# Fused attention and token mixer on one core: g_norm as one row, batch 1 per head pair, planned SyncE issues, and u of two batches turned by DMA

## The chip, the core and the metric

The kernel runs on one core of a Trainium2 chip. The metric is the device time of one execution in microseconds. Every run of a changed kernel was made beside runs of the kernel before on the same chip. The profile of an execution shows five compute engines (PE for matmuls and transposes by matmul, DVE, ACT, POOL, and SP, which here only issues transfers) and 16 DMA engines. Two words are used below. A run is called *slow* when it took over 1.5% longer than the fastest run of the same kernel, and *fast* otherwise; slow runs are left out of all ratios, but not out of the medians. *Half clock* is something else: in these traces PE's granted clock falls to 0.50 during or after some of PE's idle times, and stays there for 3.4 or 6.8 us while the kernel runs.

## The reference, cut to what matters

```python
# B=8 batches, H=8 heads, S=576 tokens, D=64; all inputs float32
def attention(q, k, v, g_norm):
    kv  = einsum('bhsd,bhse->bhde', k, v)
    out = einsum('bhsd,bhde->bhse', q, kv)
    rms = sqrt(mean(out*out, axis=-1, keepdims=True) + 1e-6)
    return out / rms * g_norm                      # g_norm has D elements

def mixer(x, w_theta, w_tok_r, w_tok_i, w_ch):     # x: (8, 576, 512)
    theta = x @ w_theta
    yr = einsum('ts,bsd->btd', w_tok_r, x * cos(theta))
    yi = einsum('ts,bsd->btd', w_tok_i, x * sin(theta))
    u  = x + yr + yi
    return u + maximum(u @ w_ch, 0)

# reference: x = attention(...) with heads side by side, result = mixer(x, ...)
```

## The kernel before

The kernel does not write its instructions in a loop. It adds every step of all eight batches as a task to an object called `Weave`: the engines that can do it with an assumed cost, the tasks it needs, the buffers it makes and uses, a priority (`due`), and, for a transfer, an assumed DMA time. While the kernel is built, `Weave.run` plays this through on a clock of its own and emits each task when its engine takes it. What comes out is a *fixed order for each engine*. On the chip nothing is decided any more: each engine takes its instructions in that order, and if the next one is not ready, all behind it wait.

```python
class Weave:
    RATE = 0.335e6          # bytes per us: a load of 256 KB is taken to need 0.78 us
    BACKLOG = 3.5           # at most so many us of transfers queued ahead
    ...
    def run(self):
        ...
                if dma is not None:
                    at = max(at, dma_free - self.BACKLOG)
        ...
            if dma is not None:
                (first, size, packed) = dma
                begin = max(start + first, dma_free)
                dma_free = begin + size / self.RATE / packed   # one server, one after the other
                end = dma_free + 0.35
            done[name] = end
...
    SP = ("SP", 0.1, 0.1)                                      # cost of an issue on SP
...
            weave.add((kind, b, hp), [SP], due(...), part(kind, src), ...,
                      dma=dma(size, 1.0), load=True)           # q, k, v: 0.78 us
...
                          dma=dma(T * H * D * 4, 0.45), load=True)   # last 64 tokens: 0.87 us
...
            weave.add(("qT", b, j), [SP], due("turn_q", b, j), fn, ...,
                      dma=dma(128e3, 0.24))                    # DMA transpose of q: 1.59 us
...
        weave.add(("out", b, ti), [...], at, store, ...,
                  dma=dma(n * P * 4, 0.9))                     # store: 0.87 us, of the last rows 0.43
```

Per batch: loads of q, k, v by head pair; q cast to 16 bit (`qcast`, DVE) and turned by DMA transposes (`qT`); kv; raw attention product, its norm (`sq` ACT, `ss` DVE, `rt` POOL, `x` DVE); transposes of x (`xTps`); `th` = x @ w_theta; cos and sin; `z` (DVE); the token mix `y` (576 matmuls in all); `uT`; u turned back by PE (`ups`); `vps` = u @ w_ch; result `ot` and its store. PE is filled with useless matmuls (`warm`) while it has nothing to do at the head.

```python
MIX_AFTER = 5                       # the mixer weights are loaded behind this head pair
...
            for r in range(P // D):                            # g_norm as a column
                nc.gpsimd.dma_start(out=gcol[r * D:(r + 1) * D, :], in_=g_norm.unsqueeze(1))
...
            for (half, r) in parts:                            # last 64 rows: two stores
                nc.sync.dma_start(out=out[b, SF:S, r * n:(r + 1) * n], in_=t[half])
```

Of the kernel before, what the change touches and what calls it, by code (L numbers as in the profile page):

```python
# [18 lines left out]
PERIOD = 24.57  # L19
START = 4.0  # L20
DUE = {
    "load": (-15.33, 2.93),
    "theta": (25.64, 0),
    "mixers": (14.15, 5.87),
    "wch": (40.71, 0.59),
    "wT": (22.86, 0.63),
    ("phase", 0): (15.82, 0),
    ("mix", 0): (31.46, 3.57),
    ("channel", 0): (44.52, 6.51),
    "first": (-5.15, 0),  # L30
    "cast": (16.13, 1.47),
    "turn_q": (5.73, 0),
    "attention": (1.6, 3.69),
    "norm": (12.64, 4.53),
    "turn": (15.9, 4.83),
    "phase": (19.49, 4.62),
    "mix": (45.0, 2.9),
    "channel": (62.48, 5.74),
# [4 lines left out]
    "rt": 6, "x": 9, "xT": 3, "pt": 2, "f": 2, "fa": 2, "tr": 2, "uT": 2, "u": 3, "ot": 3,  # L43
# [3 lines left out]
MIX_AFTER = 5  # L47
WCH_AFTER = 7


class Weave:
# [8 lines left out]
    SLACK = {"PE": 0.053, "ACT": 0, "DVE": 0.124, "POOL": 0.1, "SP": 0.05}  # L60
    MARGIN = {"PE": 0.051, "ACT": 0, "DVE": 0.444, "POOL": 0.1, "SP": 0.0}
    RATE = 0.335e6
    BACKLOG = 3.5
    BEGIN = {"PE": 1.6, "ACT": 2.2, "DVE": 1.7, "POOL": 2.5, "SP": 0.7}
    WARM = 40.0
# [19 lines left out]
    def run(self):  # L85
        done, free, last = {}, dict(self.BEGIN), {}
        dma_free = 0.0
# [21 lines left out]
        while ready:  # L109
            best = {}  # L110
            for t in ready:
                (name, engines, due, fn, needs, makes, uses, dma) = t
                if any(not self.slots[tag] for (tag, _) in makes):
                    continue
                at = max([done[n] for n in needs], default=0.0)
                for (tag, _) in makes:
                    at = max(at, min(self.slots[tag]))
                if dma is not None:
                    at = max(at, dma_free - self.BACKLOG)
                for (e, cost, lat) in engines:  # L120
                    start = max(free[e], at + self.MARGIN[e])
                    if name[0] == "warm" and start > self.WARM:
                        continue
                    best.setdefault(e, []).append((start, due, at, t, cost, lat))
            picks = []
            for (e, c) in best.items():
                first = min(x[0] for x in c) + self.SLACK[e]
                (start, due, at, t, cost, lat) = min(
# [3 lines left out]
                    (max(free[o], at) + k for (o, k, _) in t[1] if o != e), default=1e9  # L132
# [3 lines left out]
                picks.append((start, due, e, at, t, cost, lat))  # L136
            if not picks:
                break
            (_, _, e, at, t, cost, lat) = min(picks, key=lambda x: x[:3])
            (name, engines, due, fn, needs, makes, uses, dma) = t  # L140
            start = max(free[e], at)
            free[e] = start + cost
            end = start + lat
            if dma is not None:
                (first, size, packed) = dma
                begin = max(start + first, dma_free)
                dma_free = begin + size / self.RATE / packed
                end = dma_free + 0.35
# [35 lines left out]
def kernel(  # L184
# [78 lines left out]
    gcol = const.tile([P, 1], FP32, tag="gcol")  # L263
    wth = wpool.tile([P, NK, C], FP16, tag="wth", name="wth")
# [7 lines left out]
    def act(n, operands=0, small=False):  # L272
        cost = 0.1 + n / 1200.0 + 0.09 * operands
        return ("ACT", cost, cost + 0.14)

    def dve(cost):
        return ("DVE", cost, cost + 0.14)

    def pe(cost):
        return ("PE", cost, cost + 0.22)  # L280

    SP = ("SP", 0.1, 0.1)

    def dma(size, packed=1.0, first=1.7):
        return (first, size, packed)


    def idle_work(n):
# [9 lines left out]
        weave.add(("warm", n), [("PE", 0.22, 0.25)], 1e6, fn, makes=[("mm", name)])  # L298

    def load(b, hp):  # L300
        pair = slice(2 * hp, 2 * hp + 2)
        whole = P * 2 * NF * D * 4

        def part(kind, src):
            def fn(e):
                if kind == "q" or b > 0:
# [26 lines left out]
        for (i, (kind, src)) in enumerate((("q", q), ("k", k), ("v", v))):  # L333
            size = P * 2 * NF * D * 4 if kind == "q" or b > 0 else P * NS * D * 4
            weave.add((kind, b, hp), [SP], due("load", b, hp) + 0.01 * i, part(kind, src),
                      makes=[(kind, f"{kind}{b}_{hp}")], dma=dma(size, 1.0), load=True)
        if hp == (0 if b else HP - 1):
            for (i, (kind, src)) in enumerate((("kl", k), ("vl", v), ("ql", q))):
                if b == 0 and kind != "ql":
                    continue  # L340
                weave.add((kind, b), [SP], due("load", b, hp) + (0.04 if b else -0.04) + 0.01 * i,
# [4 lines left out]
                          dma=dma(T * H * D * 4, 0.45), load=True)  # L346

    def load_weights():


        def chunk(name, src, at):
            rows, cols = src.shape

            def fn(e):
# [4 lines left out]
            weave.add(name, [SP], at, fn, makes=[("wst", name)],  # L359
                      dma=dma(P * cols * 4, 1.0), load=True)  # L360

        def cast(name, of, out, src, at, scale=1.0, pool=True):
# [14 lines left out]
            on = [act(n), dve(0.06 + n / 1900.0), ("POOL", 0.17 + n / 960.0, 0.2 + n / 960.0)]  # L377
            weave.add(name, on[2:] if pool else on[:2], at, fn, needs=[of], uses=[of])
# [3 lines left out]
        for kc in range(NK):  # L382
            chunk(("wst", kc), moe_w_theta[kc * P:(kc + 1) * P, :], at + 0.01 * kc)
            cast(("wth", kc), ("wst", kc), wth[:, kc, :],
                 lambda kc=kc: st["wst", kc][:, 0:C], due("theta", 0, kc), FOLD, False)
# [17 lines left out]
        def fetch(e):  # L403
            for r in range(P // D):
                nc.gpsimd.dma_start(out=gcol[r * D:(r + 1) * D, :], in_=g_norm.unsqueeze(1))

        def gain(e):
            nc.vector.tensor_scalar(
                out=gcol[:], in0=gcol[:], scalar1=math.sqrt(D), scalar2=None, op0=ALU.mult
            )  # L410
        weave.add("gain", [("POOL", 1.3, 9.0)], -100.0, fetch)
        weave.add("gcol", [dve(0.1)], due("first", 0, 1), gain, needs=["gain"])

        def table(e):
            nc.scalar.activation(out=warm[:], in_=pio2_t[:], func=AFT.Sin)
        weave.add("sin", [("ACT", 1.5, 1.6)], due("first", 0, HP + 2), table,
                  needs=[("rt0", hp) for hp in range(HP + 1)])

    def mixer_step(n):
# [28 lines left out]
        weave.add(("wT", n), [act(S), dve(0.65)], at, keep, needs=[("wTps", n)], uses=[name])  # L448


    def cast_q(b, hp):
# [11 lines left out]
        at = due("cast", b, hp) if b else due("first", b, hp)  # L463
        weave.add(("qc", b, hp), [dve(0.33)], at, whole,
                  needs=[("q", b, hp)], makes=first,
                  uses=[f"q{b}_{hp}"] + more)
        if hp == 0:
            weave.add(("qcl", b), [dve(0.33)], at + (0.1 if b else 9.0), tail,
                      needs=[("ql", b)], uses=[f"ql{b}", f"qc{b}"])

    def turn_q(b):
        for j in range(NT):
            def fn(e, j=j):
                if j == 0:
# [6 lines left out]
            weave.add(("qT", b, j), [SP], due("turn_q", b, j), fn,  # L481
# [3 lines left out]
                      dma=dma(128e3, 0.24))  # L485

    def turn_q_by_pe(b, hp):
        name = f"qTps{b}_{hp}"
        pair = slice(2 * hp, 2 * hp + 2)

        def turn(e):
            pq = st[name] = ps("tp", [P, SX], FP16, name)
            for j in range(NT):
                nc.tensor.matmul(
                    pq[:, j * P:(j + 1) * P], qcast[b % 2][:, j, pair, :], ident16[:],
                    is_transpose=True, start=(j == 0), stop=(j == NT - 1),
                )

        def keep(e):
            if hp == 0:  # L500
                st["qT", b] = sb("qT", [P, HP, S], FP16, f"qT{b}")
            t = st["qT", b][:, hp, :]
            if e == "ACT":
                nc.scalar.copy(out=t, in_=st[name][:, 0:S])
            else:
                nc.vector.tensor_copy(t, st[name][:, 0:S])

        at = due("attention", b, hp) - 0.02
        weave.add((name,), [pe(0.3)], at, turn, needs=[("qc", b, hp), ("qcl", b)],
# [527 lines left out]
```

## Time and profile before

| | |
|---|---|
| time, median of 3 runs | 231.53 us (231.21 to 233.05) |
| span of the profiled run | 230.3 us |
| PE busy | 220.8 us, of which 23.4 us are warm matmuls |
| mean granted clock | 1.000 |
| first y / theta of batch 1 | 44.3 us / 53.8 us |

The warm matmuls of the kernel before in two stretches (0 to 25 and 25 to 60 us) and in sum; the columns are stretch, length, busy time of PE, DVE and ACT, clock, DMA share, GB/s:

```profile
0.00:25.00 25.00, 15.22 (x51) 0.06 (x1) 0.41 (x2) 1.00 0.93 261
25.00:60.00 35.00, 8.15 (x30) 0.00 (x0) 0.00 (x0) 1.00 0.99 291
sum 250.00, PE 23.38 DVE 0.06 ACT 0.41; mean PE 3.90 DVE 0.01 ACT 0.07
```

The chain of waits of the kernel before between 20 and 50 us: start, duration, what.

```profile
17.36 7.20 DMA vl<-in_v_dram
...
25.26 2.70 PE th L806 x12
...
33.41 0.87 PE wTps L432 x10
34.28 0.97 PE warm L293 x4
...
44.39 2.07 PE y L893 x18
```

The loads bound the first 25 us; after them, filler and transposes of the mixer weights (`wTps`) fill PE until the first y.

Waits of the kernel before: engine and line, what it waited for, us in total, times, longest.

```profile
DVE qcast L453 <- DMA q<-in_q_dram: 4.9, 2, 2.7
DVE qcast L459 <- DMA ql<-in_q_dram: 1.9, 1, 1.9
```

From 100 to 160 us PE is busy 59.89 of 60 us. The engines hardly ever wait for a load.

### The profile page before, as it was taken

To read this page: it belongs to the slowest core of one execution; us is meant where nothing else is said; L and a number is where in the kernel's file an instruction comes from. 1 tells how busy PE (TensorE), PEld (TensorE's weight loads), DVE (VectorE), ACT (ScalarE), POOL (GpSimd) and SP (SyncE) were. 2 spreads that over 40 slices of the span, in tenths; PEclk is the share of its full clock that TensorE was granted. 3 is DMA by queue.
4 is the path that set the end of the run, shared out by engine and by line. 5 is a ranking of instruction groups with operands and counts; after the bars stand their busy time and mean duration, and the time that the engine had idled before them with its cause. 6 is when DMAs were issued, how large, how long until landed. Compare 5 with 4: busy or idle time off the path is not lost.

```text
span 230.3 us, 5955 instructions
## 1 busy us (share of the span) xinstructions
PE 220.8 (96%) x2342; PEld 145.8 (63%) x2342; DVE 185.2 (80%) x368; ACT 157.3 (68%) x298; POOL 88.0 (38%) x108
## 2 busy tenths in 40 slices
PE   7999999999996999999999999999999999999992
PEld 2674555786754665677667766865675668655861
DVE  2268599279997798799999997998799989987553
ACT  2477687327995688767896877589849797877031
POOL 8000197436513670464266033543275336430000
PEclk9999999999999999999999999999999999999999
DMA  5899999999749996974899467996894412103214
GB/s 184 291 344 239 291 254 313 330 272 335 127 124 260 340 162 159 331 235 82 190 317 353 90 151 213 318 195 155 234 306 122 117 57 93 48 23 137 71 46 159
DMA packets 59931, 46.42 MB, mean 202 GB/s; under 512 B 29056, under 2 KB 52608, under 8 KB 59904
## 3 DMA queue, kind: packets, MB, share of 16 engines
q1 hardware_dynamic: 59840, 46.05, 71.9%
q8 instruction: 18, 0.29, 0.6%
q14 instruction: 9, 0.07, 0.1%
q0 software_dynamic: 64, 0.00, 0.0%
HBM read 33.06 MB, written 9.44 MB: 185 GB/s over the span
## 4 chain that ended last, share of the span: by engine, by line
PE 73%; DMA 9%; DVE 6%; ACT 5%; POOL 3%; issue 1%; SPq 1%; DVEq 0%
PE y L893 27%; PE vps L937 11%; PE th L806 11%; PE kv L524 6%; DMA wst<-in_moe_w_theta_dram 4%; PE xTps L775 4%; PE ups L928 4%; PE warm L293 3%; DMA vl<-in_v_dram 3%; PE raw L572 3%; DMA v<-in_v_dram 2%; POOL rt L594 2%; ACT tr L849 2%; DVE x L606 2%; PE wTps L432 2%; PE th L811 1%
## 5 line engine op out<-in xcount | busy, mean ns | idle before, releaser
L893 PE MATMUL y<-wT,z 128*128 128x320 f16 (+1 forms) x576 | 79.1, 286 | 2.2 <-DVE z L859 2.2
L893 PEld LDWEIGHTS <-z 128*128 128x128 f16 x576 | 54.0, 98 | 19.1 <-DVE z L859 2.8
L594 POOL TENSOR_TENSOR rt<-ss,mhalf 128x8 f32<-128x8 f32 x35 | 61.0, 1744 | 2.9
L590 POOL TENSOR_SCALAR ss<-ss 128x8 f32<-128x8 f32 x35 | 9.5, 271 | 85.2 <-DVE ss L583 84.6
L901 DVE SCALAR_TENSOR_TENSOR uT<-y,gcol,xT 128x256 f16<-128x256 f32 (+1 forms) x64 | 32.7, 512 | 7.9 <-PE y L893 7.6
L937 PE MATMUL vps<-wch,uT 128*128 128x512 f16 (+1 forms) x192 | 37.7, 344 | 0.0
L818 ACT ACTIVATE pt<-th,magic_t 128x512 f32<-128x512 f32 (+1 forms) x40 | 25.7, 642 | 16.6 <-PE th L806 13.3
L806 PE MATMUL th<-wth,xT 128*128 128x512 f16 x128 | 32.7, 380 | 0.0
L784 ACT ACTIVATE xT<-xTps,gcol 128x512 f16<-128x512 f16 (+1 forms) x36 | 22.9, 635 | 13.3 <-PE xTps L775 13.0
L944 ACT COPY u<-ups 128x512 f16<-128x512 f16 (+1 forms) x40 | 21.0, 537 | 14.9 <-PE ups L928 14.6
L859 DVE TENSOR_TENSOR z<-x,tr 128x1024 f16<-128x1024 f16 (+1 forms) x40 | 27.0, 674 | 3.4 <-ACT tr L849 1.7
L948 DVE SCALAR_TENSOR_TENSOR ot<-vps,u 128x512 f32<-128x512 f32 (+1 forms) x40 | 25.2, 633 | 4.1 <-PE vps L937 2.6
L822 DVE SCALAR_TENSOR_TENSOR f<-pt,th 128x512 f32<-128x512 f32 (+1 forms) x40 | 25.2, 629 | 4.0 <-ACT pt L818 3.7
L606 DVE TENSOR_TENSOR x<-raw,rt 128x512 f16<-128x512 f32 x36 | 24.7, 685 | 3.0 <-POOL rt L594 2.4
L583 DVE TENSOR_REDUCE ss<-sq 128x8 f32<-128x512 f32 x36 | 24.3, 680 | 2.3 <-ACT sq L579 2.0
L293 PE MATMUL warm<-kvbd 128*128 128x512 f16 x81 | 23.4, 410 | 2.0 <-DVE pio_t L250 1.5
L841 ACT ACTIVATE tr<-fa,pio_t 128x512 f16<-128x512 f32 x32 | 23.0, 720 | 0.5 <-DVE fa L829 0.3
L841 ACT ACTIVATE tr<-f 128x512 f16<-128x512 f32 x32 | 20.2, 630 | 3.4 <-DVE f L822 3.2
L579 ACT ACTIVATE sq<-raw 128x512 f32<-128x512 f32 x36 | 21.1, 591 | 1.2 <-PE raw L572 0.9
L937 PEld LDWEIGHTS <-uT 128*128 128x128 f16 (+1 forms) x192 | 14.1, 102 | 8.1 <-issue 0.4
L524 PE MATMUL kv<-v,k 128*64 128x64 f32 x448 | 19.0, 227 | 0.0
L524 PEld LDWEIGHTS kv<-v,k 128*64 128x64 f32 x448 | 15.3, 137 | 5.6 <-issue 4.2
(80 smaller groups left out, 243.4 us busy)
## 6 DMA issues: line engine op xcount, KB each, us to landing
q<-in_q_dram SPq DMA_DIRECT2D x32, 256.0 KB, 5.1
out_dram<-ot SPq DMA_DIRECT2D x32, 256.0 KB, 3.6
k<-in_k_dram SPq DMA_DIRECT2D x28, 256.0 KB, 5.1
v<-in_v_dram SPq DMA_DIRECT2D x28, 256.0 KB, 5.5
k<-in_k_dram SPq DMA_DIRECT2D x4, 288.0 KB, 6.2
v<-in_v_dram SPq DMA_DIRECT2D x4, 288.0 KB, 6.4
wmix<-in_moe_w_tok_r_dram SPq DMA_DIRECT2D x4, 288.0 KB, 5.5
wmix<-in_moe_w_tok_i_dram SPq DMA_DIRECT2D x4, 288.0 KB, 4.0
```

The costliest lines, as they stand in the source:

```text
L293: nc.tensor.matmul(t[:], kv_bd[1][:, 0, :], kv_bd[1][:].rearrange("p h c -> p (h c)"), start=True, stop=True,)
L524: nc.tensor.matmul(kvp[r * D:(r + 1) * D, hp, :], st["k", b, hp][:, r, j, :] if j < NF else st["kl", b][:, 2 * hp + r, :], st["v", b, hp][ ...
L594: nc.gpsimd.tensor_tensor(out=r[:], in0=t[:], in1=mhalf[:], op=ALU.pow)
L606: nc.vector.tensor_tensor(out=t[:].rearrange("p (h e) -> p h e", h=H), in0=st[raw][:].rearrange("p (h e) -> p h e", h=H), in1=st[rt][:].un ...
L806: nc.tensor.matmul(t[:], xT[:, kc, :], wth[:, kc, :], start=(kc == 0), stop=(kc == NK - 1),)
L818: nc.scalar.activation(out=t[:], in_=st[th][:], func=AFT.Identity, bias=magic_t[:])
L822: nc.vector.scalar_tensor_tensor(out=t[:], in0=st[pt][:], scalar=MAGIC, in1=st[th][:], op0=ALU.subtract, op1=ALU.subtract,)
L841: nc.scalar.activation(out=t[:, which, :], in_=src[:], func=AFT.Sin, scale=-RAD, bias=0.0 if bias is None else bias[:],)
L859: nc.vector.tensor_tensor(out=t[:], in0=xb.unsqueeze(1).broadcast_to((P, w, C)), in1=st[tr][:, 0:w, :], op=ALU.mult,)
L893: nc.tensor.matmul(t[:], z[:, kc * P:(kc + 1) * P], wT[m][:, cols], start=(m == 0), stop=(m == NM - 1),)
L901: nc.vector.scalar_tensor_tensor(out=st["uT", b][:, kc, cols], in0=st[y][:], scalar=gcol[:], in1=st["xT", b][:, kc, cols], op0=ALU.mult, o ...
L937: nc.tensor.matmul(t[half], uT(kc), wch[:, kc, r * n:(r + 1) * n], start=(kc == 0), stop=(kc == NK - 1),)
```

## The change

Its intent is to take filler out of the head, to take work off PE and DVE, and to plan SP's issues and the transfers with durations closer to those of the chip. Cut to its core:

```diff
-MIX_AFTER = 5
+U_FROM = 5
+MIX_AFTER = 3                       # mixer loads ahead of batch 1
 class Weave:
-    RATE = 0.335e6
-    BACKLOG = 3.5
-    WARM = 40.0
+    LANES = 8                        # at most 8 transfers in flight
+    WARM = 56.4
...                                    # DUE, PERIOD, SLACK, MARGIN retuned; URGENT, AHEAD added
-                    at = max(at, dma_free - self.BACKLOG)
+                    at = max(at, landed[-self.LANES])
...
-                (first, size, packed) = dma
-                begin = max(start + first, dma_free)
-                dma_free = begin + size / self.RATE / packed
-                end = dma_free + 0.35
+                (first, took) = dma
+                dma_free = max(start + first, dma_free) + took
+                end = dma_free + 0.2
+                landed.append(end)
...
-    SP = ("SP", 0.1, 0.1)
+    def sp(cost): ...                # load 0.47, tail 0.64, weights 0.38, qT 1.3, store 0.46
...                                    # assumed DMA time   before -> after
                                       # load of 256 KB      0.78 -> 0.71
                                       # load of last rows   0.87 -> 0.9
                                       # q transpose         1.59 -> 0.5
                                       # store of 256 KB     0.87 -> 0.65
                                       # weights             0.78 -> 0.66
...
-            on = [act(n), dve(...), ("POOL", ...)]
-            weave.add(name, on[2:] if pool else on[:2], ...)
+            weave.add(name, [act(n), dve(..., True), pool(n)], ...)   # any of three may cast
...
-                nc.gpsimd.dma_start(out=gcol[r * D:(r + 1) * D, :], in_=g_norm.unsqueeze(1))
+                nc.gpsimd.dma_start(out=grow[:, r * D:(r + 1) * D], in_=g_norm.unsqueeze(0))
...
+            nc.tensor.matmul(gps[:], grow[:], root_d[:], start=True, stop=True)
+            nc.vector.tensor_copy(gcol[:], gps[:])
...
-            if b == 0: first(hp) ...  # only batch 0 by head pair
+            if b < 2: by_pair(b, hp)
...
-        half, kc = divmod(i, NK)      # y: 8 chunks per batch
+        half = int(i >= NK // 2)      # y: first half in pairs of chunks, 6 per batch
+        kcs = [i - NK // 2] if half else [2 * i, 2 * i + 1]
...
-            for (half, r) in parts:
-                nc.sync.dma_start(out=out[b, SF:S, r * n:(r + 1) * n], in_=t[half])
+            nc.sync.dma_start(
+                out=out[b, SF:S, :].rearrange("t (r c) -> r t c", r=len(parts)), in_=t[:]
+            )
...
+                nc.sync.dma_start_transpose(      # u of batches 5 and 6, 8 for each
+                    out=ub[:, 2 * half:2 * half + 2, kc * P:(kc + 1) * P],
+                    in_=uT[:, kc, half * SH:(half + 1) * SH],
+                )
```

## The prediction

> **What bounds it now.** The page's busy row gives PE 96% (220.8 of 230.3 us), DVE 80%, ACT 68%. From 84 to 212 us the PE timeline is packed, so only less PE work helps there. Slack is at the head: 23.4 us of PE is filler (81 warm matmuls; windows of the warm tile put 15.2 us before 25 us, 8.2 us between 30 and 45 us), and 2.7 us idle between 60 and 80 us, on z and x of batches 1 and 2. PE work proper is about 197 us.
>
> The chain of waits at the head: loads until theta starts at 25.3, then filler and mixer transposes until the first y at 44.4. That y does not wait for z (last ends at 39.3) but for the mixers: their loads are issued after six head pairs (23.2 to 32.7 us), POOL alone casts them (28.2 to 38.6 us), the last wT ends near 43.9.
>
> **The change, costed.**
> 1. Mixer loads move ahead of batch 1, right behind theta's, and three engines may cast. At the 300 GB/s the page shows here, batch 0, theta and mixers (7 MB) take about 23 us (estimate); staging has six slots, so I put the last mixer at 29 to 31 us and the first y at 33 to 35. Batch 1's loads (11 us) come later; y of batch 0 (8.9 us), its channel stage (4.9 us) and kv by pair fill that. Filler falls from 23.4 to about 14 us: 9 us gained.
> 2. Batch 1 by head pair: same matmuls, but its norm chain starts with the first pair; takes perhaps 1 us of the 60 to 80 us bubble.
> 3. u of batches 5 and 6 by DMA: 32 PE transposes of the ups group go; four take 0.22 us start to start, so 8 tiles save 1.8 us of PE (and 8 x 0.58 us of ACT). 16 DMA transposes come; those of qT took SP 1.25 us each and landed in 2.5 us. The Trainium skill ("DMA: Bandwidth & Descriptors", DMA Transpose) asks for a two-byte type and an SP or ACT queue; both hold (30 already run here). DMA share is 0.2 to 0.7 there; SP order is the risk.
> 4. y's first half in pairs of chunks: 64 evacuations become 48. 256 columns took 0.48 us, 512 of the same operation 0.69: 16 x 0.27 = 4 us of DVE, mostly off the path.
> 5. g_norm as a row: nearly nothing; gcol's DVE operation at 13.7 us had no idle before it.
> 6. Issue planning, single tail store: at most 1 us.
>
> **Sum.** -9 -1 -1.8 -1, and 2 us given back to new waits: 231.5 - 11 = 220.5 us. Range 214 to 227.5. Chances: faster by over 2% 0.86, within 0.12, slower 0.02.
>
> **Right** if: warm matmuls fall to 12 to 16 us; the first y starts before 36 us; mixer casts end before 33 us, on ACT, DVE and POOL; the ups group has 32 fewer full-size transposes; PE from 84 us stays packed. **Wrong** if: y still starts near 44 us; warm stays above 20 us; PE idles at 45 to 60 us on batch 1's loads; a DVE ot waits for the transposes, or SP holds stores and loads behind them.
>
> **What would make it wrong:** DMA at the head slower than 300 GB/s; casts delaying batch 0's chain; a changed steady pace (about 24 us per batch), several us either way.

## More of the kernel before

The profile page of the kernel before, its busy part and its slices: busy time of each engine with its share of the span; then the span in 40 slices of 5.8 us, each digit the busy share in tenths. PEclk is the granted clock in tenths (9 is 90% or more).

```profile
span 230.3 us, 5955 instructions
PE 220.8 (96%) x2342; PEld 145.8 (63%) x2342; DVE 185.2 (80%) x368; ACT 157.3 (68%) x298; POOL 88.0 (38%) x108
PE   7999999999996999999999999999999999999992
PEclk9999999999999999999999999999999999999999
DMA  5899999999749996974899467996894412103214
```

PE is full nearly everywhere, and never at half clock. The DMA engines are full for the first 60 us and have pauses later: the loads run ahead of the work.

The steady part, all engines, in two windows: PE, PEld, DVE, ACT, POOL busy, clock, DMA share, GB/s.

```profile
60.00:100.00 40.00, 37.09 (x440) 25.20 (x439) 35.05 (x71) 31.05 (x59) 16.28 (x16) 1.00 0.90 224
100.00:160.00 60.00, 59.89 (x658) 40.88 (x657) 56.04 (x112) 46.69 (x87) 26.23 (x26) 1.00 0.77 206
```

The timeline of SP at the end shows the two stores of the last 64 rows:

```profile
226.70 1.11 SPq L960 DMA_DIRECT2D out_dram<-ot  x2
```

## The result, and the profile after

| | before | after |
|---|---|---|
| median | 232.04 us (231.21 to 233.05, 4 fast runs) | 249.73 us (247.38 to 252.28, 2 fast and 2 slow runs) |
| span of the profiled run | 230.3 us | 245.6 us |
| mean granted clock | 1.000 | 0.955 |
| warm matmuls | 23.4 us | 9.7 us |
| first y / theta of batch 1 | 44.3 / 53.8 us | 35.7 / 55.0 us |

The change made the kernel slower: the ratio is 1.0674, with a 95% interval of 1.0587 to 1.0761. A ratio here is the mean time of one kernel's fast runs over that of the other's fast runs of the same rounds, so it is not quite the ratio of the medians quoted: the two fast runs after are 247.38 and 248.08 us. The result is correct.

The profile page after:

```profile
span 245.6 us, 5784 instructions
PE 215.3 (88%) x2255; PEld 145.0 (59%) x2255; DVE 182.1 (74%) x368; ACT 151.5 (62%) x292; POOL 83.8 (34%) x98
PE   6498979999968968794999999399999999999990
PEclk9979998999999999998699999679999999999998
DMA  6997899999899969989998994639312225134432
```

PE has less to do (215.3 us instead of 220.8) and yet the span is 15.3 us longer. PE's row has holes, and in or just behind each of the three deepest (4, 4 and 3 tenths) the clock's digit is below 9. The DMA row shows fewer pauses up to 140 us than before: the loads no longer run ahead.

The warm matmuls after (the same columns), and the two steady windows:

```profile
0.00:25.00 25.00, 7.47 (x19) 0.06 (x1) 0.20 (x1) 0.93 0.88 272
25.00:60.00 35.00, 2.20 (x6) 0.00 (x0) 0.20 (x1) 0.95 1.14 288
sum 250.00, PE 9.67 DVE 0.06 ACT 0.40; mean PE 1.61 DVE 0.01 ACT 0.07
```

```profile
60.00:100.00 40.00, 33.78 (x426) 23.02 (x425) 30.32 (x60) 26.64 (x52) 12.81 (x14) 1.00 0.99 230
100.00:160.00 60.00, 51.56 (x497) 34.92 (x498) 49.18 (x97) 41.20 (x77) 27.24 (x27) 0.90 0.99 216
```

The filler did go, 13.7 us of it. But from 100 to 160 us PE is busy 51.56 us instead of 59.89 and its mean clock there is 0.90, while the DMA share rose from 0.77 to 0.99. The waits after:

```profile
DVE qcast L479 <- DMA q<-in_q_dram: 12.3, 14, 4.0
DVE qcast L485 <- DMA ql<-in_q_dram: 10.0, 5, 3.6
PE y L935 <- DVE f L855: 7.5, 2, 3.9
PE gps L430 <- DMA grow<-in_g_norm_dram: 2.6, 1, 2.6
```

DVE's waits for q (6.8 us before: 4.9 and 1.9) are 22.3 us now. How such a wait reaches PE is seen in the chain of waits after, from 108 us on:

```profile
108.45 0.29 SPq L1011
108.78 4.32 DMA q<-in_q_dram
113.13 0.43 DVE qcast L479
113.55 0.60 DVE ss L580
114.15 0.60 DVE z L892
114.75 0.61 DVE f L855
```

and in the timelines of DVE and PE of the same microseconds (start, duration, instruction, and in brackets the idle time before it with what ended it):

```profile
108.35 0.75 DVE L946 SCALAR_TENSOR_TENSOR uT<-y,gcol,xT 128x512 f16<-128x512 f32 x1
113.13 0.43 DVE L479 CAST qcast<-q 128x512 f16<-128x512 f32 x1 [4.03 <-DMA q<-in_q_dram]
...
110.76 1.03 PE L839 MATMUL th<-wth,xT 128*128 128x512 f16 x4
115.40 2.56 PE L935 MATMUL y<-wT,z 128*128 128x320 f16 x9 [3.62 <-DVE f L855]
```

SP issued the load of q only at 108.78. DVE's fixed order has the cast of that q next, so DVE stands still for 4.03 us with `ss`, `z` and `f` of another batch behind the cast, all of them ready. PE in turn waits 3.62 us for them, and the clock is 0.50 from 114.4 to 121.2 us, from within this idle time on. The same happens again at 153 us: DVE waits 3.60 us for the last rows of q of batch 7 (`ql`, issued at 149.5 us), PE waits for `f` behind that cast, and the clock is 0.50 from 155.3 to 162.2 us.

```profile
157.35 2.93 PE L935 MATMUL y<-wT,z 128*128 128x256 f16 x13 [3.88 <-DVE f L855]
```

Added over the trace, stretches of more than 0.6 us from the start of one matmul to the start of the next are 4.2 us before and 25.2 us after, and PE ran about 20 us at half clock, by which some 10 us of full clock are lost (the mean clock, 0.955 of 245.6 us, gives 11).

When the loss occurs can be read by asking when PE has done a given amount of matmul work, with filler left out. The columns are times of the kernel before; the entries are how much later (+) or earlier (-) the other kernel has done the same work.

| at (us) | 45 | 75 | 85 | 95 | 105 | 115 | 145 | 155 | 205 |
|---|---|---|---|---|---|---|---|---|---|
| after | -3.3 | -1.4 | -0.7 | +2.3 | +3.9 | +10.0 | +14.9 | +16.0 | +14.6 |

The kernel after is ahead at 45 us, loses everything between 75 and 155 us, and keeps its pace from then on. The first DMA transpose of u is issued at 186.6 us, behind the loss; no `ot` waited for one.

The end of SP's timeline after:

```profile
239.79 0.52 SPq L1015 DMA_DIRECT2D out_dram<-ot  x1
```

SP needs 0.52 us for one store instead of 1.11 us for two. But the span ends at 245.6, 5.8 us after that issue, where it ended 3.6 us after the issue before (226.70 and 230.3). The 128 packets of 1024 bytes of the last rows took from 240.95 to 244.22 us with two or three in flight; before, from 227.83 to 228.91 us with up to 16 in flight, most often 13 or 14.

### The profile page after: what moved, and what is told of

Its sections match the earlier page's. It is cut to its first block, busy times and chain, and to the rows that moved or that the text cites. A ratio compares the mean times of both kernels' runs of the same rounds, so it can differ in the third digit from the quotient of the medians.

```text
span 245.6 us, 5784 instructions
## 1 busy us (share of the span) xinstructions
PE 215.3 (88%) x2255; PEld 145.0 (59%) x2255; DVE 182.1 (74%) x368; ACT 151.5 (62%) x292; POOL 83.8 (34%) x98
## 4 chain that ended last, share of the span: by engine, by line
PE 47%; DMA 17%; SPq 13%; DVE 10%; POOL 4%; ACT 3%; issue 3%; DVEq 0%; POOLq 0%; ACTq 0%
PE y L935 19%; DMA q<-in_q_dram 9%; PE vps L993 8%; PE th L839 6%; SPq L503 6%; PE kv L521 5%; SPq L329 4%; DMA grow<-in_g_norm_dram 2%; DMA vl<-in_v_dram 2%; DMA k<-in_k_dram 2%; DVE ss L580 2%; POOL rt L591 2%; DVE ot L1004 2%; PE xTps L786 2%; PE raw L569 2%
## 5 line engine op out<-in xcount | busy, mean ns | idle before, releaser
L935 PE MATMUL y<-wT,z 128*128 128x320 f16 (+1 forms) x576 | 82.7, 295 | 9.7 <-DVE f L855 7.5
L935 PEld LDWEIGHTS <-z 128*128 128x128 f16 x576 | 56.0, 100 | 29.3 <-issue 11.3
L591 POOL TENSOR_TENSOR rt<-ss,mhalf 128x8 f32<-128x8 f32 x31 | 53.2, 1717 | 2.6
L851 ACT ACTIVATE pt<-th,magic_t 128x512 f32<-128x512 f32 (+1 forms) x40 | 25.4, 641 | 16.0 <-PE th L839 11.5
L946 DVE SCALAR_TENSOR_TENSOR uT<-y,gcol,xT 128x320 f16<-128x320 f32 (+1 forms) x48 | 29.3, 611 | 6.2 <-PE y L935 6.0
L874 ACT ACTIVATE tr<-f 128x512 f16<-128x512 f32 x32 | 19.9, 629 | 13.1 <-DVE f L855 13.1
L1000 ACT COPY u<-ups 128x512 f16<-128x512 f16 (+1 forms) x32 | 16.8, 530 | 15.9 <-PE ups L984 15.6
L479 DVE CAST qcast<-q 128x512 f16<-128x512 f32 x32 | 13.6, 428 | 13.3 <-DMA q<-in_q_dram 12.3
L603 DVE TENSOR_TENSOR x<-raw,rt 128x512 f16<-128x512 f32 x32 | 21.8, 683 | 0.8 <-POOL rt L591 0.2
L795 ACT ACTIVATE xT<-xTps,gcol 128x512 f16<-128x512 f16 (+1 forms) x32 | 20.0, 632 | 2.9 <-PE xTps L786 2.8
L1004 DVE SCALAR_TENSOR_TENSOR ot<-vps,u 128x512 f32<-128x512 f32 (+1 forms) x32 | 19.7, 617 | 2.8 <-PE vps L993 2.2
L892 DVE TENSOR_TENSOR z<-x,tr 128x1024 f16<-128x1024 f16 (+1 forms) x32 | 19.7, 616 | 0.7 <-ACT tr L882 0.3
L839 PEld LDWEIGHTS <-xT 128*128 128x128 f16 x128 | 11.6, 99 | 12.0 <-issue 1.2
```

What stands on the lines that cost most here:

```text
L591: nc.gpsimd.tensor_tensor(out=r[:], in0=t[:], in1=mhalf[:], op=ALU.pow)
L603: nc.vector.tensor_tensor(out=t[:].rearrange("p (h e) -> p h e", h=H), in0=st[raw][:].rearrange("p (h e) -> p h e", h=H), in1=st[rt][:].un ...
L839: nc.tensor.matmul(t[:], xT[:, kc, :], wth[:, kc, :], start=(kc == 0), stop=(kc == NK - 1),)
L851: nc.scalar.activation(out=t[:], in_=st[th][:], func=AFT.Identity, bias=magic_t[:])
L874: nc.scalar.activation(out=t[:, which, :], in_=src[:], func=AFT.Sin, scale=-RAD, bias=0.0 if bias is None else bias[:],)
L935: nc.tensor.matmul(st[y][:, c, :], z[:, kc * P:(kc + 1) * P], wT[m][:, cols], start=(c == 0 and m == 0) if open_sums else m == 0, stop=m = ...
```

## The experiments

The prediction had counted the planning as "at most 1 us" gained. Theories after reading the traces:

- **A.** The new assumed transfer times are too short. The planner puts casts, transposes and issues where their data will not be there yet, and as every engine works in order, one late load stops all. The head's gain is lost this way.
- **B.** The DMA transposes of u, and SP's time for them, delay stores and loads.
- **C.** The row of g_norm, which PE must wait for at 8.8 us, starts a delay that is never made good.
- **D.** The order by head pair in batch 1 does harm.
- **E.** The single store of the last rows costs at the end.

The expectations below use other letters for some of these: there B is the row of g_norm (C here), C the order by head pair (D here), and D the DMA transposes of u (B here). A is the same.

All eighteen runs gave correct results. The table gives them all. *Planned* is the start of PE's last product (of the last `vps`) on the planner's own clock, printed while the kernel is built; *chip* is the start of the same instruction in the trace; *late* is the difference. *DMA sum* is what the planner assumed for the transfers of one steady batch (12 loads, 3 loads of last rows, 5 q transposes, 4 stores and one of last rows): for the kernel before 12 x 0.7825 + 3 x 0.869 + 5 x 1.592 + 4 x 0.869 + 0.435 = 23.9 us.

| kernel | median us | ratio (95%) | DMA sum | planned | chip | late |
|---|---|---|---|---|---|---|
| before | 232.04 | 1 | 23.9 | 219.4 | 225.5 | 6.1 |
| after | 249.73 | 1.0674 (1.0587, 1.0761) | 16.7 | 209.7 | 238.6 | 28.8 |
| a_u8 | 249.53 | 1.0699 (1.0618, 1.0780) | 16.7 | 211.7 | 241.2 | 29.5 |
| a_gcol | 250.80 | 1.0779 (1.0713, 1.0845) | 16.7 | 211.4 | 247.2 | 35.8 |
| a_oldplan | 239.53 | 1.0301 (1.0236, 1.0366) | 23.9 | 220.6 | 228.2 | 7.6 |
| b_newplan | 247.74 | 1.0664 (1.0592, 1.0736) | 16.7 | 214.0 | 241.7 | 27.7 |
| a_took | 237.68 | 1.0214 (1.0172, 1.0255) | 23.9 | 219.9 | 227.0 | 7.0 |
| a_back | 247.22 | 1.0601 (1.0526, 1.0677) | 16.7 | 210.6 | 235.4 | 24.8 |
| a_op_u8 | 240.36 | 1.0253 (1.0167, 1.0340) | 23.9 | 222.1 | 232.4 | 10.2 |
| a_op_pair0 | 237.84 | 1.0224 (1.0171, 1.0277) | 23.9 | 221.4 | 227.0 | 5.6 |
| b_tail1 | 234.58 | 1.0098 (1.0068, 1.0127) | 23.9 | 219.4 | 225.9 | 6.5 |
| a_tail2 | 246.23 | 1.0563 (1.0502, 1.0624) | 16.7 | 209.7 | 239.1 | 29.3 |
| a_took_tail2 | 233.12 | 1.0048 (1.0001, 1.0094) | 23.9 | 219.9 | 225.4 | 5.4 |
| a_took_tail2_early | 235.33 | 1.0147 (1.0104, 1.0190) | 23.9 | 219.9 | 228.5 | 8.5 |
| b_mix3 | 232.82 | 1.0013 (0.9963, 1.0063) | 23.9 | 221.0 | 226.3 | 5.2 |
| a_meas | 239.88 | 1.0307 (1.0249, 1.0364) | 20.1 | 214.7 | 231.0 | 16.3 |
| n_t4 | 237.06 | 1.0193 (1.0136, 1.0250) | 20.1 | 212.4 | 230.4 | 18.0 |
| n_t2 | 237.27 | 1.0182 (1.0123, 1.0241) | 20.1 | 213.2 | 230.1 | 16.9 |
| a_took_early2 | 237.13 | 1.0177 (1.0138, 1.0217) | 23.9 | 221.9 | 229.2 | 7.3 |
| n_m2 | 231.12 | 0.9922 (0.9883, 0.9961) | 22.8 | 218.2 | 224.8 | 6.6 |

(The profiled runs of a_gcol, a_op_u8 and a_tail2 are slow ones, so their chip and late columns are too high by some microseconds; their ratios come from fast runs.)

The same comparison, made for SP (the planner's clock against SP's timeline), shows where the lateness builds up. The table has how much later than planned SP issued the first load of q of each batch (us):

| batch | 1 | 2 | 3 | 4 | 5 | 6 | 7 |
|---|---|---|---|---|---|---|---|
| before | 0.2 | 2.0 | 4.1 | 3.4 | 3.3 | 2.8 | 3.7 |
| after | 5.8 | 7.1 | 9.7 | 12.0 | 17.0 | 21.4 | 26.1 |
| b_newplan | 3.0 | 6.4 | 8.8 | 13.1 | 17.0 | 20.9 | 23.8 |
| a_took_tail2 | 2.8 | 2.8 | 3.7 | 3.0 | 2.7 | 2.3 | 3.3 |

In the plans of all four the median cast of q stands 0.3 to 0.8 us behind the planned landing of its data, so the casts of the kernel before have no more room than the others. What differs is whether SP and the transfers keep to the plan. The q of the wait at 108.78 us was planned to be issued at 88.7 us and cast at 92.1.

### a_u8: u of batches 5 and 6 by PE again (theory B)

```diff
 # the kernel after
-U_FROM = 5
+U_FROM = 8
```

> The changed kernel with u of batches 5 and 6 turned by PE again, nothing else. Theory A (the new planning of SyncE issues and transfers leaves SP and DMA no slack, so every engine's order is built for data that comes later than planned): the loss arises before 163 us, ahead of the first u transpose, so this stays within 5 us of the changed kernel (243 to 253 us). Rival D (the DMA transposes of u cause the loss): back to about 233 us or less.

Measured: 249.53 us, 1.0699. Theory B falls as the cause of the loss: without a single DMA transpose of u the time is the same.

### a_gcol: g_norm as a column again (theory C)

```diff
 # the kernel after
-    ... grow[:, r * D:(r + 1) * D], in_=g_norm.unsqueeze(0)   # and the matmul gps
+    ... gcol[r * D:(r + 1) * D, :], in_=g_norm.unsqueeze(1)   # and DVE's product with sqrt(D)
```

> The changed kernel with g_norm fetched as a column twice and scaled on DVE, as before. Theory B (the PE waits in order for the row of g_norm, 2.8 us at 8.6 us, and falls to half clock for 3.4 us after it): theta of batch 0 starts 2 to 4 us earlier, and 2 to 5 us of the total come back (243 to 247). Theory A: no more than that comes back, the stalls between 60 and 160 us stay. If g_norm were the main cause: below 237 us.

Measured: 250.80 us, 1.0779. This was a miss: removing PE's wait for the row gained nothing. The run does not isolate the row, though: its plan orders many other tasks anew as well. The wait is real, as the timeline of PE after shows,

```profile
11.42 0.35 PE L430 MATMUL gps<-root_d,grow 1*128 1x1 f32 x2 [2.62 <-DMA grow<-in_g_norm_dram]
```

and the clock is at 0.50 from 12.0 to 15.4 us. Theory C cannot be the main cause, because the kernel after is still 3.3 us ahead at 45 us in the table of work done. Whether it would be further ahead without the wait, this does not show (see a_took_tail2_early).

### a_oldplan and b_newplan: the planning alone (theory A)

a_oldplan is the kernel after with the whole transfer model of before (rate, backlog, SP at 0.1 us, landing). b_newplan is the kernel before with only the new model; its work, its priorities and its stores are untouched.

```diff
 # b_newplan: the kernel before with
-    BACKLOG = 3.5
+    LANES = 8
-                dma_free = begin + size / self.RATE / packed
-                end = dma_free + 0.35
+                dma_free = max(start + first, dma_free) + took
+                end = dma_free + 0.2
 # and the new issue costs and DMA times at each weave.add; a_oldplan is the reverse, in the kernel after
```

> The changed kernel with the transfer planning of before (SP issue 0.1 us, 335 KB per us, backlog 3.5 us, transposes 1.6 us of DMA time each), all else as changed. Theory A: the DVE no longer waits for q (12 us of waiting in the changed kernel falls below 6), the SP does not fall ever further behind its plan, and the total comes to 228 to 236 us. Rivals (by-pair batch 1, retuned priorities, lost filler, u transposes): stays above 243 us.

> The kernel before with only the new transfer planning (SP issue 0.47 us, 0.71 us per load, eight in flight, transposes 0.5 us of DMA), nothing else of the change. Theory A: slower than before by 5 to 15 us (237 to 247), with new waits of DVE for q and of PE behind them. Rivals: within 2% of before (228 to 236).

Measured: a_oldplan 239.53 us, 1.0301, between the two ranges that were expected; b_newplan 247.74 us, 1.0664, just above theory A's range. This shows that the planning alone is enough: put into the kernel before, it costs as much as the whole change. Its waits and its steady window look like those of the kernel after:

```profile
DVE qcast L454 <- DMA q<-in_q_dram: 18.5, 12, 4.9
DVE qcast L460 <- DMA ql<-in_q_dram: 8.4, 5, 3.1
...
100.00:160.00 60.00, 52.28 (x533) 35.34 (x531) 45.50 (x91) 37.91 (x71) 23.10 (x22) 0.94 0.85 205
```

By work done it is 3.7 us late at 75, 13.0 at 115 and 16.3 at 205 us. The undoing takes the waits for q from 22.3 us to 4.1 us, but leaves 3% unexplained at this point.

### a_took and a_back: which part of the planning

```diff
 # a_took: the kernel after with the DMA times of before, everything else of the new planning kept
-                      ... dma=dma(0.71), load=True)     # loads
+                      ... dma=dma(0.7825), load=True)
-                      dma=dma(0.5))                     # q transposes
+                      dma=dma(1.592))
-                  uses=[ot], dma=dma(0.65 if full else 0.4))
+                  uses=[ot], dma=dma(0.869 if full else 0.435))
 # (weights, last rows and u transposes in the same way)
 # a_back: the kernel after with only the pacing of before
-                    at = max(at, landed[-self.LANES])
+                    at = max(at, dma_free - self.BACKLOG)
```

> The changed kernel with only the assumed DMA time per transfer put back to the values of before (a load 0.78 instead of 0.71 us, a q transpose 1.59 instead of 0.5, a store 0.87 instead of 0.65, u transposes 0.80 instead of 0.35); SP issue costs and eight in flight stay as changed. If the assumed DMA times are what broke the plan: about as fast as with the whole old planning, 236 to 242 us. If it is the pacing (eight in flight) or the SP costs: stays at 245 us or more.

> The changed kernel with only the pacing put back (a transfer may be issued when the backlog is under 3.5 us, not when fewer than eight are in flight). If the pacing is the cause: 236 to 242 us. If the assumed DMA times are: stays at 245 us or more.

Measured: a_took 237.68 us, 1.0214; a_back 247.22 us, 1.0601. It is the assumed DMA times: by the ratios, which leave the slow runs out, 4.6 of the 6.7% come back with them (1.0674 to 1.0214). The pacing gives 0.7%, within the intervals of the two, and SP's issue costs, which a_took keeps, are not needed for the recovery. Which of the assumed times does it was not tested; of the 7.2 us per batch by which their sum fell, 5.5 us are the q transposes.

### a_op_u8 and a_op_pair0: what is left with the old planning (theories B and D)

```diff
 # both: a_oldplan, and
-U_FROM = 5                          # a_op_u8
+U_FROM = 8
-            if b < 2: by_pair(b, hp)   # a_op_pair0: batch 1 by row tiles as before
+            if b < 1: by_pair(b, hp)
```

> The old transfer planning in the changed kernel (239.5 us) and u of batches 5 and 6 turned by PE again. There a DVE ot waited 3.8 us for a u transpose and PE lost 2 us at 216 us behind it. If that wait is what the u transposes cost now that the plan is sound: 1 to 3 us faster than 239.5. If they pay for themselves (1.8 us of PE saved): 1 to 2 us slower.

> The old transfer planning in the changed kernel and batch 1 by row tiles again (q turned by PE, as before), without the four priority entries of batch 1 by pair. Theory A: by-pair is worth little either way, within 3 us of 239.5. Rival C (by-pair of batch 1 is the rest of the loss): 2 us or more faster, near 234.

Measured: 240.36 us, 1.0253, and 237.84 us, 1.0224, beside 1.0301 for a_oldplan. Neither interval stands clear of a_oldplan's (1.0236 to 1.0366); two of the four runs of a_op_u8 are slow. By the ratios both are one to two microseconds faster than a_oldplan, which these runs do not tell from the noise and from the new plans.

### b_tail1, a_tail2 and a_took_tail2: the store of the last rows (theory E)

```diff
 # b_tail1: the kernel before with the single store
-            for (half, r) in parts:
-                nc.sync.dma_start(out=out[b, SF:S, r * n:(r + 1) * n], in_=t[half])
+            nc.sync.dma_start(out=out[b, SF:S, :].rearrange("t (r c) -> r t c", r=len(parts)), in_=t[:])
 # a_tail2, a_took_tail2: the reverse, in the kernel after and in a_took
```

> The kernel before with only the store of the 64-row tail made one DMA (outermost dimension 2) as in the change. In the changed kernel's trace that last store kept 2 or 3 packets in flight for 3.3 us, the two stores of before 13 or 14 for 1.1 us in all. If the store runs on two DMA engines only: 2 to 4 us slower than before (234.5 to 236.5), the last landing over 3 us after its issue. If one store is as good as two, as the prediction assumed: 0 to 1 us faster.

> The changed kernel with two tail stores again, nothing else. If the single tail store only lengthens the end: 2 to 3 us faster (246 to 248). If the eight of them also hold up loads in the steady state: 4 us or more faster. Theory A: the large loss between 100 and 160 us stays, so not below 241.

> Assumed DMA times of before and two tail stores in the changed kernel. The run with the times alone was 237.7, 2.1% over before, and its last store ended 5.3 us after its issue. Expected 234 to 235.5: within 1.5% of before. If something else in the change is the rest of the loss: stays at 237.

Measured: b_tail1 234.58 us, 1.0098 in five rounds; a_tail2 246.23 us, 1.0563; a_took_tail2 233.12 us, 1.0048, the last a little better than expected. The plan of b_tail1 is the same to the end (planned 219.4), and the order of every engine is the same, so its 2.3 us are the store itself. The Trainium skill ("DMA: Bandwidth & Descriptors", section "Why a DMA increments its semaphore by 16 and not by 1") says that the number of DMA engines that a transfer uses is the largest number up to 16 that divides the slowest dimension of both access patterns that is not of size 1. The rearranged store has an outermost dimension of 2, so two engines; the traces agree, with two or three packets in flight instead of up to 16, and 3.3 us instead of 1.1. a_took_tail2 gains more over a_took, 4.5 us. The orders of these two are the same as well, but in the profiled run of a_took PE was at half clock for 6.8 us instead of 3.4 in the first 20 us, and was 2.3 us later from there to 205 us, which no store of last rows can have caused.

With both causes undone the kernel after is level with before: 1.0048 with an interval from 1.0001. Its waits and its steady window:

```profile
DVE qcast L479 <- DMA q<-in_q_dram: 2.9, 2, 2.0
...
100.00:160.00 60.00, 59.16 (x659) 40.05 (x657) 54.63 (x106) 48.72 (x91) 27.03 (x27) 1.00 0.95 213
```

So the loss is accounted for to within a per cent (the interval ends at 1.0094). What is not there is the gain: this kernel has all the work of the change but the single store, its filler is 9.9 us, and by work done it is ahead by 4.1 us at 45 and 3.3 us at 85 us, then level to within 1 us from 105 us on.

### b_mix3: the head alone

```diff
 # the kernel before
-MIX_AFTER = 5
+MIX_AFTER = 3
```

> The kernel before with the mixer loads moved ahead of batch 1 (right after the theta weights), nothing else. The prediction's step 1: the first y starts 8 us earlier and the total falls by several us. Rival: theta of batch 1 needs all four pairs of batch 1, whose last load comes after the same bytes in either order, so it still starts at 53 to 56 us and the total stays within 1% of before.

Measured: 232.82 us, 1.0013 (0.9963 to 1.0063). The first y came at 39.7 us instead of 44.3, the filler fell from 23.4 to 20.7 us, and nothing was gained. Its chain of waits between 43 and 54 us says why:

```profile
43.17 8.37 DMA vl<-in_v_dram
51.55 0.14 issue
51.68 0.34 PE kv L524 x4
...
53.66 0.86 PE th L806 x4
```

Theta of batch 1 starts at 53.7 us, as before (53.8). Its loads stand behind the mixers' now, and whichever comes first, the same bytes must have landed before batch 1 is complete. An earlier y of batch 0 only changes what PE does in the meantime.

### a_meas, n_t4 and n_t2: the transfer times as measured

In the traces a load of 256 KB is 256 packets of 1024 bytes at 52 ns, which is 0.83 us on 16 engines, and SP needs 1.25 us for each DMA transpose. a_meas gives the planner what was measured; it also has the two stores and fetches the row of g_norm first. n_t4 and n_t2 are a_meas with other priorities, found by an offline search over plans.

```diff
 # the kernel after, with two stores of the last rows and the row of g_norm issued first
-   load 0.71, last rows 0.9, q transpose 0.5, store 0.65, u transpose 0.35
+   load 0.83, last rows 0.8, q transpose 0.9, store 0.69, u transpose 0.45
 # n_t4, n_t2: this, with other numbers in DUE, SLACK and MARGIN, and U_FROM = 4
```

> The changed kernel with two tail stores, the row of g_norm fetched before the memsets (and the planner told when it lands), and DMA times in the planner as measured in these traces (load 0.83, q transpose 0.9, store 0.69, u transpose 0.45 us). The plan then ends at 219 us against 224 with the old times. If a plan with true times is kept by the chip: 225 to 230. If slack in the plan is needed as well as truth: 231 to 238.

> As a_meas, with priorities searched anew offline on that plan and on copies of it with transfers made late at random (plan 216.8 us; u of batches 4 to 6 by DMA). If plan and chip differ by the usual 5 to 6 us: 222 to 228, faster than both kernels. If the order is again too tight: 230 or more.

> As n_t4 from another search (plan 217.6 us, best of the searches where transfers are slowest). 222 to 229 if plans with true times hold.

Measured: 239.88, 237.06 and 237.27 us (1.0307, 1.0193, 1.0182). Better than the kernel after and worse than before; all three are outside the ranges expected if plans with measured times hold. Measured mean times are not enough: on the chip these kernels fall 16 to 18 us behind their plans. The column *late* orders all kernels by one number. At 16.7 us of planned DMA per batch they end 25 to 30 us late (a_gcol, with a slow profile, 35.8), at 20.1 us 16 to 18 us late, and at 22.8 us and more 5 to 10 us late. How many microseconds the DMA engines are really busy for one batch is no fixed number: in the kernel before the share is 0.74 over the 23.8 us from the y of one batch to that of the next (96.2 to 143.7 us for two), which makes 18 us, but in a_took_tail2, which is not slower by much, it is 1.00 over 25.4 us (94.3 to 145.2 us). The share adds up the times of packets that overlap, so that it can exceed 1 (1.14 above).

### a_took_tail2_early and a_took_early2: the row of g_norm once more (theory C)

```diff
 # a_took_tail2, with the fetch of grow ahead of POOL's memsets
+    for r in range(P // D):
+        nc.gpsimd.dma_start(out=grow[:, r * D:(r + 1) * D], in_=g_norm.unsqueeze(0))
-        weave.add("grow", [("POOL", 1.3, 5.0, False)], -100.0, fetch)
+        weave.add("grow", [("POOL", 0.05, 5.5, False)], -100.0, lambda e: None)   # early2 alone
```

> The same, and the row of g_norm fetched by POOL before its memsets instead of after them (it was issued at 4.5 us and landed at 11.3, PE waiting 2.8 us and dropping to half clock). Expected: that wait under 0.5 us, theta of batch 0 at 23 to 24.5 us instead of 26, total 231 to 234, level with before. If the wait at 9 us is later absorbed: as fast as without.

> The changed kernel with the old assumed transfer times, two tail stores, and the row of g_norm fetched before POOL's memsets, this time with the planner told that the row needs 5.5 us to land, so that PE's matmul on it is not put first in PE's order. Same kernel without the early row: 233.1 us (1.0048 of before). Theory 'PE's wait of 2.6 us on the row and the half-clock window after it cost time at the end': 231 to 232.5 us, ratio 0.995 to 1.001, no wait of PE on grow over 0.5 us and no half clock before 14 us. Rival 'PE is ahead there and gives the time to warm matmuls, so the wait costs nothing': 233 us, ratio 1.003 to 1.007, with the wait gone and more warm matmuls.

Measured: 235.33 us, 1.0147, and 237.13 us, 1.0177, beside 1.0048 for a_took_tail2. Both missed. In the first, the planner no longer knew that the row must land; it put the matmul on it at the top of PE's order, where PE waited 6.1 us:

```profile
PE gps L428 <- DMA grow<-in_g_norm_dram: 6.1, 1, 6.1
```

All other tasks stand in the same order as in a_took_tail2, so here two traces can be compared directly. PE has done the same work 2.5 us later at 20 us and 3.8 us later at 55 us, theta of batch 1 starts at 59.6 instead of 55.8 us, and the 3.8 us are still there at 205 us. A delay at the head that reaches theta of batch 1 is thus not made good. In the second the wait is gone (PE takes the row at 10.8 us without idle time before it), and the kernel is still 1.3% slower: the plan that came out has two new gaps in front of y, at 65 and 95 us, with half clock behind them. The line of its page:

```profile
PEclk9999999999979999899999999999999999999999
```

That is a lesson about most of the runs here: a small edit of one task can give a new order of many others (in this second kernel only some 210 of PE's 328 tasks keep their order among each other), and the time may then move by a per cent or more for reasons that have nothing to do with the edit. Differences below about 1.5% between kernels with different plans say little of the part that was edited. b_tail1, a_took_tail2 and a_took_tail2_early are not touched by this (same orders as the kernels they are compared with, but for the two tasks moved in the last), nor are the two main results, which are several times as large. What g_norm as a row is worth could therefore not be measured; that PE's wait for it costs time at the end is likely after a_took_tail2_early, but not shown.

### n_m2: a plan with room for late transfers

```diff
 # as n_t4, but
-   last rows 0.8, q transpose 0.9, store 0.69, u transpose 0.45
+   last rows 0.87, q transpose 1.3, store 0.8, u transpose 0.65
 # and with priorities from a further search, which replayed a plan's fixed orders with late transfers; U_FROM = 5, MIX_AFTER = 3, WCH_AFTER = 5
```

> An attempt at a kernel better than both: the changed kernel with two tail stores, the early row, DMA times in the planner a little above those measured, and priorities, slacks and U_FROM searched offline for a plan that stays short when the actual durations are jittered. If slack in the plan against late transfers is what was lost, its PE gaps over 0.6 us sum to under 10 us, q casts wait under 5 us in all, and it takes 229 to 233 us. If the steady pace depends on something that the planner does not model (transposes slowed beside loads), it stays at 235 to 238 us as the two earlier searched kernels did.

Measured in five rounds: 231.12 us (229.92 to 231.99), beside 232.67 us for the kernel before in the same rounds; ratio 0.9922, interval 0.9883 to 0.9961. It is the only kernel that beats the kernel before, by 0.8%. It contains every part of the change except the single store, and it fetches the row of g_norm early. Its page:

```profile
span 229.6 us, 5868 instructions
PE 215.4 (94%) x2285; PEld 143.0 (62%) x2285; DVE 181.1 (79%) x359; ACT 153.4 (67%) x300; POOL 85.5 (37%) x99
PE   7879999999998999999989999999999999999892
PEclk9999999999999999999999999999999999999998
```

It ends 6.6 us behind its plan, as the kernel before does (6.1), its waits for q are 6.1 and 1.5 us (under 5 in all were expected), stretches of over 0.6 us between the starts of matmuls are 10.0 us in all, and there is no half clock before the last product. Its filler is 17.6 us, against 9.9 in a_took_tail2, which is slower: less filler is not more speed. By work done it is 2.5 us ahead at 45 us, 1.1 at 115, 0.1 at 145, and 0.1 us *behind* at 205 us: here too the head's gain is gone. What it has left at the end is that PE has about 1.8 us less to do (32 transposes of u fewer, of which four take 0.22 us from start to start). That this is where the 0.8% come from is argued from these sums, not shown by a run of its own. It also differs from n_t4 in two things at once, the assumed times and the priorities; that the times are the cause rests on the column *late* over all kernels, not on this pair.

## Why the prediction was wrong, point by point

Two steps failed. Step 6 counted the new planning as a gain of at most 1 us, and the planning alone cost 6.6%. Step 1 counted 9 us of filler as 9 us of time, and the same move in the kernel before was worth nothing (1.0013).

1. **Step 1, "9 us gained" from the mixer loads.** What it named came: warm matmuls fell to 9.7 us (12 to 16 predicted), the first y came at 35.7 us (33 to 35 predicted), and ACT, DVE and POOL cast, the last cast of mixer weights started at 28.4 us. But it was worth nothing: b_mix3 is at 1.0013. The failed term is the equation of filler removed with time gained. The same loads precede batch 1 in either order, theta of batch 1 stays at 53.7 to 55.0 us (55.8 in a_took_tail2, 56.4 in n_m2), and whatever PE is ahead at 45 us (2.5 to 4.1 us in the three kernels of the change that the table or the text gives) is gone by 105 to 145 us. The planner says the same: with the DMA times of before it plans the last product of the changed kernel at 219.9 or 220.6 us (a_took, a_oldplan), no earlier than that of the kernel before (219.4).
2. **Step 6, "at most 1 us" for issue planning and the single store.** This step failed most. The transfer planning alone costs 6.6% in the kernel before (b_newplan), and undoing only its assumed DMA times gives back 4.6 of 6.7% in the kernel after (a_took). The prediction treated a model's numbers as bookkeeping; they fix the order on every engine. The single store cost 2.3 us (b_tail1) instead of a gain.
3. **Step 5, g_norm as a row, "nearly nothing".** PE waits 2.6 us for it and runs at half clock for 3.4 us after it, because the matmul stands in PE's order. What that costs at the end stays open: of three attempts to remove it, two got new plans and one made PE wait longer. That last one shows at least that such a delay can be carried to the end (3.8 us).
4. **Step 3, u by DMA, 1.8 us of PE.** The count was right: the ups matmuls went from 160 to 128. In the kernel after no `ot` waited for one, SP's 1.2 us for each did no visible harm, and a_u8 shows no cost. A gain of 1 to 2 us is compatible with n_m2 but was not shown separately.
5. **Step 2, batch 1 by pair, 1 us, and step 4, y in pairs of chunks.** Step 2's gain is not shown; a_op_pair0 without it was no slower than a_oldplan. Step 4's count was right (48 evacuations of y instead of 64, 29.3 us of DVE instead of 32.7); no run undoes it.
6. **"PE from 84 us stays packed"** was given as a sign of being right, and "a changed steady pace, several us either way" as what would make the prediction wrong. The second is what happened, at 17 us rather than several, between 75 and 155 us (-1.4 to +16.0 in the table of work done).

Open: why planned transfers of 20.1 us per batch, taken from measured means, still end 16 us late. A mean says nothing of bursts. In the kernel after the small packets are slower in the middle of the kernel (256 bytes: 29 to 33 ns from 60 to 160 us, 20 to 30 ns before), but this alone is not the reason: in a_took_tail2 and n_m2, which end 5 to 7 us late, they take 29 to 32 ns from 60 to 135 us as well.

## What to carry to other kernels

When an order is fixed at build time for engines that work in order, the assumed times are part of the program: an optimistic transfer time puts an instruction ahead of its data, and everything behind it stops. Plan transfers with room above their measured mean (here 22.8 us per batch kept to its plan where 20.1 did not, though the priorities differed too), compare the plan's clock with the trace (by how much is the last product late, and where does that grow), and test a change of the model in the old kernel by itself. Filler on PE is not time to be gained until the chain behind it, here the loads of the next batch, is shorter as well; and a merged store should be looked at for how many DMA engines its outermost dimension lets it use.

## What the Trainium skill lacked or had wrong

- "DMA: Bandwidth & Descriptors", section "Why a DMA increments its semaphore by 16 and not by 1": the rule for the number of engines agrees with the traces, but the page has no measured time for such a transfer. Here a store of 128 KB with an outermost dimension of 2 took 3.3 us with two or three packets in flight; the same bytes as two stores took 1.1 us. It was 1.0% of the kernel (b_tail1).
- The same page, section "DMA Transpose (X-bar)": the section has no figure for transposes beside loads, nor for the issuing engine (elsewhere the page has sequencer cycles of transposes, in a comparison of chips). Here each held SP for about 1.25 us, and packets of 256 bytes (those of the transposes and of the loads of the last rows) took 20 to 24 ns between 85 and 185 us in the kernel before and 29 to 33 ns in the busier one up to 185 us.
- The same page, section "Anatomy of one DMA — SWDGE (gpsimd) path", gives about 2.0 us of fixed cost. The two transfers of 256 bytes for g_norm, issued from POOL, landed 3.8 and 4.5 us after the start of their issue at the very start (n_m2), and 6.1 and 6.5 us after it at 4 to 5 us, behind queued loads (the kernel after). Of this, POOL's issue itself took 0.5 to 0.7 us.
- "TensorE: Matmul & The Clock Gate", "Part 1: The HAM clock gate", gives a window of 3413 ns, and the traces agree (half clock lasted 3.4 us twice and 6.8 us twice in the kernel after, before its last product). It puts the fall to half rate after at least one idle window of about 3.4 us. In a_took_early2 PE was idle for 1.99 us, from 65.1 to 67.1 us, and the clock fell to 0.50 at about 66.6 us and stayed there until 70 us. So a shorter gap can be enough; the gaps of 1.7 to 1.9 us at 68, 89 and 99 us in the kernel after had no such fall behind them.
- No page speaks of the risk that was decisive here: orders fixed from assumed durations on engines that work in order. The runs show its size: 6.6% of the kernel from the transfer planning alone (b_newplan), 4.6% given back by the assumed DMA times alone (a_took).
